# Four w3·w_out sums open at once, six places for w3, and 40 products on zeros ahead of the first head

## The chip, the cores and the metric

The kernel runs on one core of a Trainium2 chip. The metric is the device time of one execution in microseconds (us), the median of three runs. Of the kernel before, one execution was also taken by the hardware profiler; every duration below comes from that one.

The core has five engines that run queues of their own, in order: PE (TensorE: matrix products, whose weight loads are listed apart as PEld), DVE (VectorE), ACT (ScalarE), POOL (GpSimd) and SP (SyncE, which here only starts DMA transfers). An instruction waits for semaphores that other engines or transfers raise; everything behind it on its queue waits too.

## What is computed

Attention with a band and 32 global tokens over 8 batches of 8 heads, and behind it a gated block on the attention's 4,352 rows:

```python
# per head: 512 local and 32 global queries, head_dim 64
s_g  = scale * q_g @ k_all.T                 # global tokens see all
s_ll = where(|i - j| <= 32, scale * q_l @ k_l.T, -1e9)
s_l  = concat([scale * q_l @ k_g.T, s_ll])
out  = concat([softmax(s_g) @ v_all, softmax(s_l) @ concat([v_g, v_l])])
# all heads of a token side by side: x is (8*544) x 512
a = x @ w1;  b = x @ w2                      # 512 x 1024 each
h = a * b @ w3                               # 1024 x 1024
y = h @ w_out                                # 1024 x 512
```

The kernel folds `w3 @ w_out` into one 1024 x 512 matrix first (called w34), so that the gated product is multiplied once. Weights arrive as 64-bit words, which ACT and DVE turn into 32-bit floats; products that need it are done with a high and a low part of an operand.

## The kernel before, in words

**The early part.** The weights come in units of 512 KB (16 of `w3`, 8 of `w_out`, 8 of `w12`, the latter holding w1 and w2 side by side) and in 16 half units (`w12s`). A unit is fetched into one of three `raw` buffers (`fetch`), unpacked in three steps (`unit`: step 0 on DVE, step 2 on ACT, step 3 on DVE), and for w12 split into high and low (steps 4 and 5). `fold(t, j)` is one product of 128 rows of w3's tile t with 128 rows of w_out; eight of them, j = 0 to 7, add up to a 128-row block t of w34 in one PSUM bank, and the trace shows each as two MATMUL instructions. Eight blocks make 64 folds. `fold(t, j)` needs the half tile of w3 (t, j // 4) and the unit j of w_out. A finished block is copied out as a high part (`w34h`, ACT) and a low part (`w34l`, DVE).

**A head n** is loaded (`kr`, `qr`, by pairs `vr`), split (`kh`, `kl`, `qs`, `vs`), scored (`s`, eight products), put through maximum (`mmax`, DVE), exponent (`exps`, ACT) and scaling by the inverse sum (`norm`, ACT or DVE), transposed (`t`), split into `PTh`, `PTl` and `G` on ACT and DVE, multiplied with v (`av`, ten products) and added up (`cb`, ACT; `sum`, DVE). The global tokens take `sg` (scores, by pairs of heads) and `tg` (transposes, by four heads). When the four pairs of a batch are there, `first` (12 products each; tiles `ap` and `bp`), a gate and `second` (tile `acc`) make the gated block; that goes on beside the heads of the next batches.

**What sets the order.** Nothing is scheduled on the chip. A planner in the program (`list_schedule`) goes through all steps with costs and due times that are written by hand, and its answer is the order in which each engine's instructions stand. `ORDER` lists the weight units, `W0 + WD * n` is the due time of the n-th, `LA` is the distance of the first eight heads, `LB` that of the later ones. `take(tag, bufs, ...)` tells the planner how many places a tile has. Before, `product(t)` puts the eight folds of one block one behind the other, w3 has two places (`w3f`), and `ORDER` brings the whole of w_out ahead of w3's tiles 1 to 7.

**The very front.** POOL clears `QG` (the high and low parts of the global queries, 128 x 512) before ACT casts the first queries into it.

## Time and profile before

| | us |
|---|---|
| median of three runs | 936.43 (933.89 to 937.55) |
| the profiled execution | 934.75 |
| its span in the trace | 933.0 |
| PE busy | 871.0 (93%) |
| ACT busy | 667.2 (72%) |
| DVE busy | 636.5 (68%) |
| POOL busy | 385.4 (41%) |

The profiled execution lies 1.7 us under the median, inside the range of the three runs. What the span does not cover of it is 1.75 us. A stretch is read by the busy time of its engines and by the clock that TensorE was granted (1.00 is 2.4 GHz, 0.5 is 1.2 GHz, and a value between is the mean of a stretch that had both). Where PE is not busy, the view of waits and the timeline name what it waited for. From 215 us to 800 us PE is busy in 99 of 100 us at the full clock, so that stretch is as long as its products.

### The profile page before, as it was taken

How to read it: one execution, taken by the hardware profiler on the slowest of the kernel's cores; microseconds unless marked ns; L12 is line 12 of the kernel's file. 1: busy time of each engine (PE TensorE's matmuls, PEld its weight loads, DVE VectorE, ACT ScalarE, POOL GpSimd, SP SyncE). 2: the span in 40 equal slices, each digit the busy share in tenths (PEclk: the TensorE clock that was granted, in tenths of full speed). 3: DMA queues.
4: the chain of work that ended last, by engine and by line, in shares of the span. 5: the costliest groups of instructions: out<-in, count | busy, mean ns of one | idle time of the engine just before them, and what ended most of it. 6: DMA issues, size and time to landing. Idle time of an engine off the chain costs nothing.

```text
span 933.0 us, 17736 instructions
## 1 busy us (share of the span) xinstructions
PE 871.0 (93%) x6016; PEld 786.1 (84%) x6016; DVE 636.5 (68%) x1683; ACT 667.2 (72%) x1779; POOL 385.4 (41%) x462
## 2 busy tenths in 40 slices
PE   3599968799999999999999999999999999999995
PEld 2355548688999999999999999999999999999994
DVE  4779887886777868786878677878786767512111
ACT  5678887897878787878887888788878877512111
POOL 4444457554544345444544454345434543200000
PEclk9789968999999999999999999999999999999998
DMA  9755533423131313131313231223121211000000
GB/s 270 238 157 162 180 122 125 140 81 90 54 100 40 98 48 105 46 99 54 98 53 95 57 99 52 85 62 94 49 89 57 91 45 36 1 23 23 1 23 22
DMA packets 38514, 78.51 MB, mean 84 GB/s; under 512 B 5784, under 2 KB 6808, under 8 KB 38424
## 3 DMA queue, kind: packets, MB, share of 16 engines
q1 hardware_dynamic: 38424, 77.39, 27.2%
q8 instruction: 47, 0.77, 0.3%
q14 instruction: 43, 0.35, 0.1%
HBM read 68.45 MB, written 8.91 MB: 83 GB/s over the span
## 4 chain that ended last, share of the span: by engine, by line
PE 79%; ACT 8%; DVE 6%; DMA 3%; issue 2%; POOL 1%; SPq 0%; ACTq 0%; POOLq 0%; DVEq 0%
PE bp L495 7%; PE bp L496 7%; PE bp L497 7%; PE acc L525 6%; PE acc L527 6%; PE acc L526 6%; PE ap L497 5%; PE ap L495 5%; PE ap L496 5%; PE w L630 5%; PE s L299 4%; PE av L379 3%; PE av L378 3%; DVE PTl L233 3%; PE t L325 3%; ACT PTh L230 2%
## 5 line engine op out<-in xcount | busy, mean ns | idle before, releaser
L495 PE MATMUL ap<-x,w12h 128*128 128x256 f32 x544 | 158.4, 291 | 0.6 <-ACT w12h L230 0.6
L497 PE MATMUL ap<-x,w12l 128*128 128x256 f32 x544 | 155.2, 285 | 1.3 <-POOL w12l L233 1.2
L495 PE MATMUL bp<-x,w12h 128*128 128x256 f32 x544 | 155.1, 285 | 0.0
L496 PE MATMUL ap<-x,w12h 128*128 128x256 f32 x544 | 154.5, 284 | 0.0
L496 PE MATMUL bp<-x,w12h 128*128 128x256 f32 x544 | 154.3, 284 | 0.0
L497 PE MATMUL bp<-x,w12l 128*128 128x256 f32 x544 | 154.2, 284 | 0.0
L307 ACT ACTIVATE P<-P,mn 128x192 f32<-128x192 f32 (+1 forms) x256 | 121.2, 475 | 13.0 <-DVE mn L303 11.5
L233 DVE TENSOR_TENSOR PTl<-t,PTh 32x96 fp32r<-32x96 f32 (+1 forms) x192 | 76.6, 399 | 76.9 <-ACT PTh L230 39.9
L233 POOL TENSOR_TENSOR kl<-kr,kh 128x608 fp32r<-128x608 f32 x56 | 84.7, 1513 | 101.2 <-ACT kh L230 81.3
L230 ACT CAST PTh<-t 32x96 fp32r<-32x96 f32 (+1 forms) x192 | 66.8, 348 | 59.2 <-PE t L328 34.1
L497 PEld LDWEIGHTS ap<-x,w12l 128*128 128x128 f32 x544 | 104.5, 192 | 2.2 <-POOL w12l L233 1.9
L496 PEld LDWEIGHTS bp<-x,w12h 128*128 128x128 f32 x544 | 104.4, 192 | 2.0
L495 PEld LDWEIGHTS bp<-x,w12h 128*128 128x128 f32 x544 | 104.4, 192 | 1.9
L495 PEld LDWEIGHTS ap<-x,w12h 128*128 128x128 f32 x544 | 104.7, 192 | 0.9 <-ACT w12h L230 0.8
L496 PEld LDWEIGHTS ap<-x,w12h 128*128 128x128 f32 x544 | 104.8, 193 | 0.1
L497 PEld LDWEIGHTS bp<-x,w12l 128*128 128x128 f32 x544 | 104.4, 192 | 0.0
L303 DVE CUSTOM_DVE_ANT_0 P<-s,cs 128x192 f32<-128x192 f32 (+1 forms) x256 | 86.0, 387 | 6.5 <-PE s L299 4.8
L233 POOL TENSOR_TENSOR qs<-qr,qs 64x512 fp32r<-64x512 f32 x46 | 61.9, 1346 | 49.7 <-ACT qs L230 37.3
L630 PE MATMUL w<-wo,w3f 128*128 128x512 f32 x128 | 64.4, 642 | 13.9 <-DVE wo L556 12.3
L299 PE MATMUL s<-kh,qs 128*128 128x192 f32 (+1 forms) x256 | 67.1, 296 | 5.3 <-POOL qs L233 2.8
L401 DVE TENSOR_TENSOR u<-av,cb 64x704 f32<-64x704 f32 x64 | 56.8, 887 | 19.2 <-ACT cb L394 18.4
L379 PE MATMUL av<-PTl,vs 128*128 128x192 f32 (+1 forms) x256 | 65.6, 280 | 0.0
(785 smaller groups left out, 2377.8 us busy)
## 6 DMA issues: line engine op xcount, KB each, us to landing
kr<-in_kd_t_dram SPq DMA_DIRECT2D x128, 152.0 KB, 2.9
raw_w<-in_w_t_dram SPq DMA_DIRECT2D x24, 512.0 KB, 4.1
kpr<-in_kp_t_dram SPq DMA_DIRECT2D x32, 272.0 KB, 2.8
out_dram<-o SPq DMA_DIRECT2D x34, 256.0 KB, 2.9
qr<-in_q_t_dram SPq DMA_DIRECT2D x64, 128.0 KB, 2.7
vr<-in_v_t_dram SPq DMA_DIRECT2D x32, 256.0 KB, 2.7
raw_wo<-in_wo_t_dram SPq DMA_DIRECT2D x8, 512.0 KB, 6.3
raw_w12s<-in_w_t_dram SPq DMA_DIRECT2D x16, 256.0 KB, 3.3
```

The lines of the kernel that those rows point to most:

```text
L230: (nc.scalar.copy if eng in (None, nc.scalar) else eng.tensor_copy)(dst, src)
L233: (eng or nc.gpsimd).tensor_sub(dst, src, f(hi))
L299: nc.tensor.matmul(st[:, e, 0:w], qs[:, 128 * e : 128 * e + 128], kk[:, o : o + w], start=(j == e % 2 == 0), stop=(j == 1), skip_group_che ...
L303: nc.vector.tensor_tensor_reduce(blk(n, e), T["st", n][:, e, 0 : WIN[e][1]], masks[e], -0.125, 3.0e38, ALU.add, ALU.min, T["mn", n][:, e : ...
L307: nc.scalar.activation(blk(n, e), blk(n, e), AF.Exp, bias=T["mn", n][:, e : e + 1], scale=-1.0, accum_out=T["sm", n][:, e : e + 1])
L379: nc.tensor.matmul(dst, v, PTl[:, j, c0:c1], start=False, stop=last, skip_group_check=True)
L401: nc.vector.tensor_add(u[r : r + 64], T.pop(("av", n))[r : r + 64, :, 0:352], T.pop(("cb", n))[r : r + 64])
L495: nc.tensor.matmul(d, wh[:, k, c, :], x[:, 0, 0:w], start=(k == m % 2 == 0), stop=False, skip_group_check=True)
L496: nc.tensor.matmul(d, wh[:, k, c, :], x[:, 1, 0:w], start=False, stop=False, skip_group_check=True)
L497: nc.tensor.matmul(d, wl[:, k, c, :], x[:, 0, 0:w], start=False, stop=(k == 3), skip_group_check=True)
L525: nc.tensor.matmul(a, gh[:, m % 2, sl], wh, start=(m == 0), stop=False)
L630: nc.tensor.matmul(T["w34", t], T["w3f", t, j // 4][:, j % 4], T["wo"][:, j], start=(j == 0), stop=(j == 7))
```

## The change

It has four parts.

1. `ORDER` is rewritten: w3's tiles 0 to 3 (first halves) alternate with w_out's units 0 to 3, then their second halves with w_out's units 4 to 7; tiles 4 to 7 follow as before. `W0` goes from -16 to -8, `WD` from 3.0 to 2.6, `LA` from 8 to 9.
2. The blocks 0 to 3 of w34 accumulate at the same time, in four PSUM banks (two of `acc`, and the banks `a` and `b` that `first` uses later). Each fold now has the due time of its own two units.
3. w3's half tiles get six places: two of `w3f`, and four buffers (`g`, `as`, `gh`, `gl`) that the gate uses later.
4. `halves`: 40 products, 256 columns wide, on `QG` while it holds zeros, as PE's first work; 8 use all 128 rows, 32 use rows 0 to 63 and 64 to 127 in turn and two banks in turn. Nothing reads what they write.

```diff
-LA, LB, LF = 8.0, 11.2, 4.0
+LA, LB, LF = 9.0, 11.2, 4.0
-W0, WD = -16.0, 3.0
+W0, WD = -8.0, 2.6
 ORDER = (
-    ('w3', 0, 0), ('wo', 0, 0), ('wo', 1, 0), ('wo', 2, 0), ('wo', 3, 0), ('w3', 0, 1), ('wo', 4, 0), ('wo', 5, 0),
+    ('wo', 0, 0), ('w3', 0, 0), ('w3', 1, 0), ('wo', 1, 0), ('w3', 2, 0), ('wo', 2, 0), ('w3', 3, 0), ('wo', 3, 0),
...
+W3F = ("w3f", "w3f", "g", "as", "gh", "gl")
+W34P = ("acc", "acc", "a", "b")
...
-                    T["w3f", a, h] = P["early"].tile([128, 4, 128], F32, tag="w3f", name=f"w3f{a}_{h}", bufs=2)
+                    tag = W3F[[u[1:] for u in ORDER if u[0] == "w3"].index((a, h)) % len(W3F)]
+                    pool, n = (P["early"], 2) if tag == "w3f" else (p1, 1)
+                    T["w3f", a, h] = pool.tile([128, 4, 128], F32, tag=tag, name=f"w3f{a}_{h}", bufs=n)
...
     def fold(t, j):
         if j == 0:
-            T["w34", t] = ps_acc.tile([128, 512], F32, tag="acc", name=f"w34_{t}")
+            tag = W34P[t % 4]
+            T["w34", t] = (ps_acc if tag == "acc" else ps_1).tile([128, 512], F32, tag=tag, name=f"w34_{t}")
...
+    def halves():
+
+        z = QG.rearrange("p a b -> p (a b)")
+        st = ps_1.tile([128, 2, 512], F32, tag="s", name="halves")
+        for r in range(8):
+            nc.tensor.matmul(st[:, 0, 0:256], z[:, 128 * (r % 2) : 128 * (r % 2) + 128], z[:, 256:512],
+                             start=True, stop=True)
+        for r in range(32):
+            h, c = 64 * (r % 2), 128 * (r // (2 if r < 16 else 4) % 2)
+            nc.tensor.matmul(st[:, r % 2, 0:256], z[h : h + 64, c : c + 128], z[h : h + 64, 256:512],
+                             start=True, stop=True)
...
-    def product(t, due):
-        take("acc", 2, ("w34", t), ("fold", t, 0))
+    def product(t):
+        due = {u: W0 + WD * n for n, u in enumerate(ORDER)}
+        due = [max(due["w3", t, j // 4], due["wo", j, 0]) + 4.0 for j in range(8)]
+        tag = W34P[t % 4]
+        take(tag, W34P.count(tag), ("w34", t), ("fold", t, 0))
...
-            add(("fold", t, j), only("PE", COST["fold"]), due + 0.1 * j, deps, fold, t, j)
+            add(("fold", t, j), only("PE", COST["fold"]), due[j], deps, fold, t, j)
...
+    add(("halves",), only("PE", 4000), -70.0, [("clear", "QG")], halves)
```

**Where it moves instructions: the front of ACT.** Before, ACT's first instructions (the names in brackets are semaphores that an instruction waits for, `PE_49` being the one that PE raises):

```order
L230 ACT_TABLE_LOAD [waits DMAHW0_49]
L230 CAST QG_77<-qgr0_97 64x4x32 [waits Pool_49]
L230 CAST QG_77<-qgr0_97 64x4x32
L554 ACTIVATE raw_w30_0_101<-raw_w30_0_101 128x512 [waits DMAHW2_49]
L554 ACTIVATE raw_wo0_0_103<-raw_wo0_0_103 128x512 [waits DMAHW3_49]
L230 CAST qs0_146<-qr0_106 64x512 [waits DMAHW4_49]
L554 ACTIVATE raw_wo1_0_108<-raw_wo1_0_108 128x512 [waits DMAHW5_49]
L230 CAST vgs_76<-vgr0_112 64x8x64 [waits DMAHW7_49,DMAHW6_49]
L230 CAST kh0_164<-kr0_119 128x608 [waits DMAHW1_49,DMAHW0_49]
```

and after the change:

```order
L233 ACT_TABLE_LOAD [waits DMAHW0_49,PE_49]
L233 CAST QG_77<-qgr0_97 64x4x32 [waits Pool_49]
L233 CAST QG_77<-qgr0_97 64x4x32 [waits PE_49]
L233 CAST qs0_163<-qr0_142 64x512 [waits DMAHW2_49]
L233 CAST vgs_76<-vgr0_144 64x8x64 [waits DMAHW4_49,DMAHW3_49]
L233 CAST kh0_176<-kr0_148 128x608 [waits DMAHW6_49,DMAHW5_49]
L557 ACTIVATE raw_wo0_0_156<-raw_wo0_0_156 128x512 [waits DMAHW7_49]
```

ACT's first instruction now waits for PE (the products of `halves` read `QG`, which ACT is to overwrite), and two of the three scalings of weight units that stood ahead of head 0's `kh` stand behind it.

**PE around the transposes of head 1.** Before, from the folds ahead of `t1` on (`w34_0`, `w34_1` are blocks of w34, `w3f0_1` is the second half of w3's tile 0):

```order
L630 MATMUL w34_0_152<-wo_93,w3f0_1_273 128x512 x2
L325 MATMUL t1_392<-cs_70,P1_72 128x128 x4
L328 MATMUL t1_392<-cs_70,P1_72 128x128 x3
L630 MATMUL w34_0_152<-wo_93,w3f0_1_273 128x512
L422 MATMUL sg2_438<-kph2_390,QG_77 128x272 x2
L422 MATMUL sg2_438<-kpl2_407,QG_77 128x272 x2
L382 MATMUL av1_446<-G_75,vgs_76 128x288
```

and after:

```order
L636 MATMUL w34_2_408<-wo_93,w3f2_0_386 128x512 x2
L636 MATMUL w34_0_261<-wo_93,w3f0_0_254 128x512
L636 MATMUL w34_1_281<-wo_93,w3f1_0_272 128x512
L636 MATMUL w34_2_408<-wo_93,w3f2_0_386 128x512
L328 MATMUL t1_439<-cs_70,P1_72 128x128 x4
L331 MATMUL t1_439<-cs_70,P1_72 128x128 x3
L636 MATMUL w34_3_453<-wo_93,w3f3_0_437 128x512 x3
L636 MATMUL w34_0_261<-wo_93,w3f0_0_254 128x512
L385 MATMUL av1_485<-G_75,vgs_76 128x288
```

Between the value products of head 0 and those of head 1 stood three folds, all of block 0; now nine stand there, of four blocks. Before `t1`, 9 folds are done where 6 were.

**ACT around the copy `cb7` of head 7.** Before:

```order
L230 CAST kh9_1195<-kr9_827 128x608
L307 ACTIVATE P0_71,sm8_1177<-P0_71,mn8_1176 128x192
L307 ACTIVATE P0_71,sm8_1177<-P0_71,mn8_1176 128x256 x2
L307 ACTIVATE P0_71,sm8_1177<-P0_71,mn8_1176 128x192
L230 CAST w12h1_84<-raw_w121_0_1074 128x512
L394 COPY cb7_1226<-av7_1207 64x704
```

and after:

```order
L233 CAST w12h2_86<-raw_w122_0_1165 128x512
L557 ACTIVATE raw_w122_1_1204<-raw_w122_1_1204 128x512
L233 CAST kh9_1251<-kr9_973 128x608
L233 CAST qs9_1266<-qr9_1025 64x512
L310 ACTIVATE P0_71,sm8_1225<-P0_71,mn8_1224 128x192
L310 ACTIVATE P0_71,sm8_1225<-P0_71,mn8_1224 128x256
L397 COPY cb7_1280<-av7_1255 64x704
```

Ahead of `cb7` ACT now works on w12's tile 2, where it was at tile 1. In all, 222 steps of the planner stand ahead of `cb7` on ACT where 208 stood: eight more `norm`, three more scalings and two more high parts of w12 units, two more copies of `tg`, one more `qs`, and two `exps` fewer.

## Rows read from the trace of the kernel before

**Rows 1.** Busy time by stretch: stretch, length, PE PEld DVE ACT POOL (instructions), clock, DMA, GB/s.

```profile
0.00:14.00 14.00, 3.15 (x4) 1.04 (x5) 4.06 (x9) 5.85 (x10) 6.47 (x11) 1.00 0.86 232
14.00:51.00 37.00, 21.68 (x88) 15.65 (x87) 27.58 (x82) 26.06 (x69) 15.66 (x15) 0.76 0.81 245
51.00:121.00 70.00, 68.26 (x260) 38.35 (x260) 58.41 (x150) 57.53 (x151) 35.66 (x42) 0.98 0.53 166
121.00:139.00 18.00, 9.21 (x44) 7.60 (x43) 14.42 (x36) 15.40 (x41) 10.07 (x12) 0.63 0.42 134
139.00:215.00 76.00, 67.33 (x454) 60.88 (x454) 61.26 (x149) 62.82 (x171) 43.74 (x49) 0.93 0.37 115
215.00:800.00 585.00, 579.08 (x4329) 549.15 (x4328) 443.49 (x1212) 471.98 (x1285) 267.96 (x326) 1.00 0.23 70
```

**Rows 2.** Waits of PE, 0 to 62 us: total us, times, longest.

```profile
PE w L630 <- DVE wo L556: 12.3, 3, 10.0
```

**Rows 3.** Timeline of the front: start us, us, engine, line, what, [idle before <- releaser].

```profile
0.74 0.52 POOL L187 MEMSET QG<- 128x512 f32 x1 [0.29 <-POOLq L1046]
2.56 1.28 ACT L230 ACT_TABLE_LOAD   x1 [2.56 <-DMA qgr<-in_qg_t_dram]
3.85 0.62 ACT L230 CAST QG<-qgr 64x128 fp32r<-64x128 f32 x2
...
13.15 0.70 ACT L230 CAST kh<-kr 128x608 fp32r<-128x608 f32 x1 [0.48 <-DMA kr<-in_kd_t_dram]
13.88 0.79 DVE L233 TENSOR_TENSOR kl<-kr,kh 128x608 fp32r<-128x608 f32 x1 [1.01 <-ACT kh L230]
14.01 1.15 PE L299 MATMUL s<-kh,qs 128*128 128x192 f32 x1
```

**Rows 4.** Timeline of PE: neighbouring 256-column products, of head 0 and of head 3.

```profile
15.65 0.41 PE L299 MATMUL s<-kh,qs 128*128 128x256 f32 x1
15.87 0.41 PE L299 MATMUL s<-kl,qs 128*128 128x256 f32 x1
...
58.00 0.28 PE L299 MATMUL s<-kl,qs 128*128 128x256 f32 x1
58.12 0.28 PE L299 MATMUL s<-kh,qs 128*128 128x256 f32 x1
```

**Rows 5.** Timeline of ACT and PE: the key cast and first score product of head 1.

```profile
26.02 0.70 ACT L230 CAST kh<-kr 128x608 fp32r<-128x608 f32 x1 [0.15 <-DMA kr<-in_kd_t_dram]
...
30.08 0.34 PE L299 MATMUL s<-kh,qs 128*128 128x192 f32 x1
```

**Rows 6.** Timeline of PE: its last long waits in the early part, and the folds behind.

```profile
36.33 0.58 PE L382 MATMUL av<-G,vgs 128*128 128x288 f32 x1 [5.10 <-DVE PTl L233]
...
47.62 0.79 PE L422 MATMUL sg<-kph,QG 128*128 128x272 f32 x2 [3.80 <-DVE mn L303]
...
50.77 4.34 PE L630 MATMUL w<-wo,w3f 128*128 128x512 f32 x6
```

**Rows 7.** Timeline of PE: four folds (eight instructions) at the full clock.

```profile
102.24 3.62 PE L630 MATMUL w<-wo,w3f 128*128 128x512 f32 x8
```

**Rows 8.** ACT's groups, 0 to 215 us: count, busy us, mean ns, idle before.

```profile
L307 ACT ACTIVATE P<-P,mn 128x192 f32<-128x192 f32 (+1 forms) x56 | 26.4, 473 | 4.7 <-DVE mn L303 4.4
L554 ACT ACTIVATE raw_w<-raw_w 128x512 f32<-128x512 f32 x24 | 15.7, 674 | 2.6 <-DMA raw_w<-in_w_t_dram 2.5
...
L317 ACT ACTIVATE P<-P,sm 128x192 f32<-128x192 f32 (+1 forms) x34 | 14.5, 472 | 0.0
...
L230 ACT CAST w12h<-raw_w 128x512 fp32r<-128x512 f32 x8 | 5.2, 656 | 0.1
```

**Rows 9.** Waits of PE, 121 to 215 us, the two longest groups.

```profile
PE av L382 <- ACT P L307: 3.1, 1, 3.1
PE s L299 <- POOL qs L233: 2.8, 1, 2.8
```

**Rows 10.** Timeline: copy `cb` of head 7 on ACT, first product of `first` on PE.

```profile
130.15 0.74 ACT L394 COPY cb<-av 64x704 f32<-64x704 f32 x1 [1.05 <-PE av L379]
...
138.92 0.47 PE L495 MATMUL ap<-x,w12h 128*128 128x256 f32 x1
```

More of the change, by code (lines that the diff above doesn't have):

```diff
@@ L48 @@
 SEEN, SEEN_PE, ISSUE, LAND, RATE = 110, 300, 480, 1900, 270.0
-LA, LB, LF = 8.0, 11.2, 4.0
+LA, LB, LF = 9.0, 11.2, 4.0
 HOLD_A, HOLD_D, HOLD_P = 400, 0, 90000
-W0, WD = -16.0, 3.0
+W0, WD = -8.0, 2.6
 ORDER = (
-    ('w3', 0, 0), ('wo', 0, 0), ('wo', 1, 0), ('wo', 2, 0), ('wo', 3, 0), ('w3', 0, 1), ('wo', 4, 0), ('wo', 5, 0),
-    ('wo', 6, 0), ('wo', 7, 0), *[('w3', t, e) for t in range(1, 8) for e in range(2)],
-    *[('w12', m, e) for m in range(MA) for e in range(2)],
-)
+    ('wo', 0, 0), ('w3', 0, 0), ('w3', 1, 0), ('wo', 1, 0), ('w3', 2, 0), ('wo', 2, 0), ('w3', 3, 0), ('wo', 3, 0),
+    ('w3', 0, 1), ('wo', 4, 0), ('w3', 1, 1), ('wo', 5, 0), ('w3', 2, 1), ('wo', 6, 0), ('w3', 3, 1), ('wo', 7, 0),
+    *[('w3', t, e) for t in range(4, 8) for e in range(2)], *[('w12', m, e) for m in range(MA) for e in range(2)],
+)
+W3F = ("w3f", "w3f", "g", "as", "gh", "gl")
+W34P = ("acc", "acc", "a", "b")
 def list_schedule(steps, after):
@@ L929, in weight @@
         if kind == "w3":
-            take("w3f", 2, ("w3f", a, e), me[3])
+            tag = W3F[[x[1:] for x in ORDER if x[0] == "w3"].index((a, e)) % len(W3F)]
+            take(tag, W3F.count(tag), ("w3f", a, e), me[3])
         if kind[:3] == "w12":
@@ L936, in weight @@
             read(me[5], ("raw", *u))
-    def product(t, due):
-        take("acc", 2, ("w34", t), ("fold", t, 0))
+    def product(t):
[3 more added lines that the diff above has]
+        take(tag, W34P.count(tag), ("w34", t), ("fold", t, 0))
         for j in range(8):
             deps = [("unit", "w3", t, j // 4, 3), ("unit", "wo", j, 0, 3)] + [("fold", t, j - 1)] * (j > 0)
-            add(("fold", t, j), only("PE", COST["fold"]), due + 0.1 * j, deps, fold, t, j)
+            add(("fold", t, j), only("PE", COST["fold"]), due[j], deps, fold, t, j)
             read(("fold", t, j), ("w34", t), ("w3f", t, j // 4))
-        add(("w34h", t), only("ACT", COST["w34h"]), due + 2, [("fold", t, 7)], fold_split, t, 0)
-        add(("w34l", t), only("DVE", COST["w34l"]), due + 3, [("w34h", t)], fold_split, t, 1)
+        add(("w34h", t), only("ACT", COST["w34h"]), due[7] + 2, [("fold", t, 7)], fold_split, t, 0)
+        add(("w34l", t), only("DVE", COST["w34l"]), due[7] + 3, [("w34h", t)], fold_split, t, 1)
         read(("w34h", t), ("w34", t))
@@ L967, in band_attention_glu_kernel @@
     for t in range(8):
-        product(t, W0 + WD * (8 + 2 * t) + 4.0)
+        product(t)
     for b in range(B):
```

## The prediction

> **What bounds the kernel now.** I read first the busy times of the engines and the granted clock by stretch [rows 1]. From 215 us to 800 us PE is busy 579.1 of 585 us at the full clock, and the order of the work there is the same in both programs. So the change is worth what it saves before 215 us, and all of that reaches the end. Before 215 us PE stands still for 10.9, 15.3, 1.7, 8.8 and 8.7 us in the five stretches, 45 us in all. On top of that comes the low clock: a granted clock c means that (1-c)/0.5 of the stretch ran at 1.2 GHz, where a product takes twice as long. That is 0.48 x 21.7/2 = 5.2 us in 14 to 51, 0.74 x 9.2/2 = 3.4 in 121 to 139, 0.14 x 67.3/2 = 4.7 in 139 to 215, and with 0.04 x 68.3/2 = 1.4 in between some 15 us. So 60 us are there to be won at most.
>
> Then I read what PE waited for. In 0 to 62 us the largest group is folds that wait for a unit of w_out [rows 2]; two long waits on its queue follow, of 5.10 us for head 0's weights and of 3.80 us for a maximum [rows 6]. From 50.8 us on PE is fed: 51 to 121 is 68.3 of 70 us busy, because folds are left over to fill it. After 121 us the folds are used up and PE waits for ACT's exponents and POOL's splits [rows 9]; ACT is 15.4 of 18 us busy there and 62.8 of 76 behind it, DVE 14.4 and 61.3 [rows 1]. So there are three regions: transfers and in-order waits up to 51, PE itself up to 121, ACT with DVE up to 215. The change moves folds out of the second into the first; what it does to ACT's order decides the third.
>
> **The front: 40 products.** They start when POOL has cleared QG, at 1.26 us [rows 3], say 1.4. PE had nothing until 9.95 us, so on PE they cost nothing; their cost is that ACT's first instruction now waits for their end, E. Behind it are queued the table load, both casts of QG, and the casts of head 0's q, of the global v and of head 0's k; DVE's low parts wait for those, PE's first scores for DVE, and SP's load of q2 (a place in a ring of three) for DVE's low part of q0. No row shows a product on 64 rows, so I bound it. Two neighbours of 256 columns are 0.22 us apart at the low clock and 0.12 at the high one [rows 4]. All 40 one after the other at the low clock take 8.8 us (E = 10.2); if two halves run at the same time and the clock is high throughout, 8 + 16 steps of 0.12 take 2.9 us (E = 4.3). A gain on PE is excluded, since they add work that nothing uses. For the clock the nearest rows are those of the run of PE that begins at 47.62 after a wait: at 50.77 its six fold instructions take 4.34 us where 2.7 would do at the full clock, so the low clock lasted there to about 54.1, 6.5 us from the start of the run [rows 6]. By that, 29 products run at the low clock and 11 at the high one if they go one by one (6.4 + 1.3, E = 9.1), and all 24 steps at the low clock if the halves go two at a time (5.3, E = 6.7). No row is nearer to the one than to the other; I take the middle, E = 7.9.
>
> The Trainium skill's page "TensorEngine Tiling (Array Packing)", section "Key Properties", says that tiles of different rows load and multiply in parallel, and that a change of tiling mode drains the engine. No run here shows either. By the first sentence E would be 6.7 instead of 7.9, and the sum below would be 1.2 us better; with halves one by one it would be 1.2 us worse.
>
> From E to head 0's first score stand the table load 1.28, two QG casts 0.62, casts of q, v and k of about 0.6, 0.6 and 0.70, and DVE's low part of k 0.79 [rows 3], with the hand-overs 4.9 us: 12.8 us, where it was 14.0 [rows 3]. So the products eat up most of what the earlier loads of head 0 bring, and no more.
>
> **Head 1.** Before, its key cast waited for its load until 26.0 us [rows 5]. Ahead of that load stand 2.1 MB less now (three full and two half weight units fewer); at 232 to 245 GB/s [rows 1] it lands some 9 us sooner, near 17. That is early enough: ACT is now last. From head 0's scores to ACT's first exponent I count 2.5 us (eight products at the low clock 1.7, the first maximum and hand-overs 0.8), then ACT has 16 instructions up to and with head 1's key cast, between 0.40 and 0.70 us each (exponents 0.473, scalings of units 0.674, of rows 0.472 [rows 8]), 8.7 us; POOL's low part adds 1.5. Head 1's scores start at 12.8 + 2.5 + 8.7 + 1.5 + 0.2 = 25.7, where it was 30.1 [rows 5].
>
> **Up to the point where PE is fed.** Behind head 1's scores stand 8 + 5 products of 0.12, two folds, 7 products. A fold is two instructions of 3.62/8 = 0.45 us [rows 7], so 0.9. Head 0's transposes end at 25.7 + 1.6 + 1.8 + 0.8 = 29.9. From there to head 0's value products it was 6.2 us (30.1, where head 1's scores followed the transposes [rows 5], to 36.3 [rows 6]) and the splits between are the same: 36.1. That is the last long wait, because behind it stand nine folds up to head 1's value products where three stood; their units (w_out 2 and 3, w3's tiles 2 and 3) come before or shortly after by the queue. Before, PE was fed from 50.8 us, and had by then done three folds, one sg, one t and two av more: 2.7 + 31 products x 0.12 = 6.4 us. So the same work was reached at 44.4 and is now reached at 36.1: **8.3 us won**. The slow clock at the start of the fed stretch (six instructions in 4.34 us where 2.7 would do [rows 6]) is paid in both.
>
> **What is given back while PE is fed.** With four blocks open, every step j needs a new unit of w_out and two to four folds follow; the units come at DVE's pace, which was 58.4 of 70 us busy [rows 1]. I give 2.0 us for short waits ahead of j = 4 to 7, from none (in the whole stretch PE stood still for 1.7 us before [rows 1], whatever it waited for) to 4 (eight units at 0.5). Places and banks cost nothing: the four buffers and two banks are first needed by the gate, behind 138.9 us [rows 10], and the folds end near 113.
>
> **ACT behind the folds.** Ahead of head 7's copy ACT gets 14 steps more: eight scalings of rows 3.8, three of units 2.0, two high parts 1.3, two copies 0.8, a q cast 0.6, less two exponents of 0.473 + 0.19: 7.2 us [rows 8]. Head 7's copy ran at 130.15 and `first` began at 138.9 [rows 10]; ACT is the last there, so nearly all of the 6.2 us left is given back at that place. But 3.3 us of the 7.2 is work on w12 that ACT did later before, and 1.9 of the row scalings come back too (over the whole program it is four more, not eight): 5.2 us returns in 139 to 215, where PE waits today. What stays on ACT is four scalings and a copy, 2.5 us. In return DVE loses those, about 2 us; since DVE was nearly as busy as ACT there, I count half, 1.0.
>
> **Sum**: -8.3 + 2.0 + 2.5 - 1.0 = -4.8 on 934.75, with the bounds of E shifting it by +2.3 or -3.6 (nearly one for one until the load at 17 us is last). Clock: PE idles less in 14 to 36 us, and of the 5.2 us lost there I count 0.5 as saved. That makes **-5.3, 929.5** for the profiled execution. It lay 1.7 us under the median; on the median of 936.4 it is **931.1**.
>
> **The rivals.**
> - *The lull keeps it*: ACT's 7.2 us more ahead of head 7 are not returned by 215 us, because the later heads wait for ACT in turn. For it: ACT is 82 to 86% busy from 121 on, the highest of the helpers [rows 1]. Against: the w12 work done early is missing later. Then -8.3 + 2.0 + 7.2 - 1.0 = -0.1: 936 on the median, between 932 and 940.
> - *Slower*: ACT is held at the front by all 40 products one after the other at the low clock (E = 10.2, +2.3), and is last from there on. Then the folds win nothing, since what PE waits for is ACT's casts at every head: the 8.3 us fall away, and the 7.2 us stand in full, less what DVE gives: 934.75 + 2.3 + 7.2 - 1.0 = 943 (945 on the median). It decides when ACT's idle time of 0 to 139 us (8.2, 10.9, 12.5 and 2.6 in the four stretches [rows 1]) doesn't fall by at least 7 us.
> - *The whole gain stays*: the halves run two at a time (E = 6.7, -1.2), no waits for units, and w12 being ready earlier saves 3 of the 8.7 us that PE stands still in 139 to 215: -8.3 - 1.2 - 3 = -12.5, 924 on the median, down to 920.
> - *The sums stand open, but PE isn't fed*: units come too late for four blocks at once (4 us instead of 2.0 and more), which leads to the first rival's time.
>
> **How the numbers follow.** What a measurement of this kernel can tell from no change is about 0.5%, 4.7 us. I give the forecast (926 to 933.5) 0.47, of which 0.34 lies under 931.7; the whole gain 0.11; the lull, with units too late, 0.25; slower by ACT 0.17. Faster by over 0.5%: 0.34 + 0.11 = 0.45. Within 0.5%: 0.13 + 0.25 = 0.38. Slower: 0.17. The range is 923 to 941: left out are about half of the whole gain and most of the slower case.
>
> **What would show it.** The table load on ACT starts near 7.9 us (4.3 to 10.2); head 0's scores near 13, head 1's near 26 with the key cast no longer waiting for a transfer; head 0's value products near 36 and no wait over 2 us on PE behind them until the last fold, which ends near 113 instead of 121, where the fed stretch ended; `first` begins between 134 and 139; from there PE is busier than 67.3 of 76 us. If head 1's scores come at 30 or later, the front is wrong; if the last fold ends near 113 and the end is still 936, the lull has kept it; if folds wait for w_out throughout, the open sums are not fed.

## The result and the profile after

The changed kernel takes 939.92 us (median of 18 runs, 936.98 to 942.78), the kernel before beside it 935.46 (18 runs, 933.67 to 937.67). The ratio is 1.0047, with an interval from 1.0036 to 1.0058: 4.5 us slower by the medians, just inside the 0.5% that the prediction called no change, and 8.8 us over its forecast of 931.1, which was faster. The profiled execution of the changed kernel took 941.34 us, its span is 939.6.

Busy time by stretch of the changed kernel, in the columns of [rows 1]:

```profile
0.00:14.00 14.00, 8.01 (x52) 7.34 (x52) 4.99 (x7) 4.71 (x8) 6.63 (x11) 0.81 0.78 237
14.00:51.00 37.00, 26.70 (x91) 14.82 (x91) 27.79 (x75) 27.92 (x74) 15.05 (x13) 0.79 0.86 225
51.00:121.00 70.00, 64.39 (x246) 36.66 (x244) 59.46 (x143) 58.75 (x154) 35.30 (x42) 0.95 0.59 180
121.00:139.00 18.00, 7.72 (x31) 6.24 (x31) 15.49 (x34) 16.41 (x42) 11.88 (x11) 0.61 0.50 160
139.00:215.00 76.00, 66.09 (x432) 60.69 (x433) 56.10 (x147) 59.28 (x168) 46.25 (x56) 0.89 0.31 91
215.00:800.00 585.00, 578.78 (x4325) 548.72 (x4325) 440.37 (x1205) 470.72 (x1281) 274.24 (x331) 1.00 0.25 72
```

PE's idle time fell in 14 to 51 us from 15.3 to 10.3 us. It rose in all three stretches behind: from 1.7 to 5.6, from 8.8 to 10.3 and from 8.7 to 9.9, and the granted clock fell in each of them. The steady stretch from 215 us on is what it was.

The front, as a timeline (start us, us, engine, line, what, [idle before <- releaser]):

```profile
1.32 2.08 PE L650 MATMUL halves<-QG 128*128 128x256 f32 x8 [1.32 <-POOL QG L190]
3.33 3.05 PE L654 MATMUL halves<-QG 64*128 64x256 f32 x32
6.46 1.28 ACT L233 ACT_TABLE_LOAD   x1 [6.46 <-PE halves L654]
9.43 0.69 ACT L233 CAST kh<-kr 128x608 fp32r<-128x608 f32 x1
10.18 0.53 PE L302 MATMUL s<-kh,qs 128*128 128x192 f32 x1 [3.80 <-ACT kh L233]
...
33.94 0.58 PE L385 MATMUL av<-G,vgs 128*128 128x288 f32 x1 [3.58 <-DVE PTl L236]
...
36.18 6.12 PE L636 MATMUL w<-wo,w3f 128*128 128x512 f32 x10
```

The 32 half products take 3.05 us, the eight full ones ahead of them 2.08. The table load waits for them until 6.46. Head 0's scores start at 10.18 (14.01 before [rows 3]), its value products at 33.94, and from the folds at 36.18 on PE is fed.

What PE waited for behind that, as the timeline shows it:

```profile
47.59 1.13 PE L636 MATMUL w<-wo,w3f 128*128 128x512 f32 x2 [1.95 <-DVE wo L559]
...
58.73 0.37 PE L385 MATMUL av<-G,vgs 128*128 128x288 f32 x1 [1.83 <-DVE PTl L236]
...
61.73 6.19 PE L636 MATMUL w<-wo,w3f 128*128 128x512 f32 x8
...
123.89 0.73 PE L328 MATMUL t<-cs,P 128*128 128x128 f32 x2 [4.04 <-ACT P L320]
...
130.92 0.58 PE L385 MATMUL av<-G,vgs 128*128 128x288 f32 x1 [2.46 <-DVE PTl L236]
...
138.91 1.49 PE L328 MATMUL t<-cs,P 128*128 128x128 f32 x4 [4.34 <-ACT P L320]
```

The eight fold instructions at 61.73 take 6.19 us, where 3.62 do at the full clock [rows 7]; the last folds end at 117.5 us (120.3 before). The transposes of heads 7 and 8 wait 4 us each for ACT's scaling of rows, and the first product of `first` starts at 142.49 (138.92 before [rows 10]).

**An account of PE's lost time.** Busy time counts slow products in full, so I also keep an account that does not: for a milestone (the scores, transposes or values of a head) I take the time at which PE starts it, less the full-clock length of all that stands ahead of it in PE's order. The lengths are distances between starts in the trace of before, once PE is fed: scores 1.0 us, transposes 0.68, values 1.16, `sg` 0.53, `tg` 0.55, a fold 0.9, twelve products of `first` or a `second` 1.44; products that nobody reads count nothing. What is left is what PE lost up to there, interpolated between milestones. Only differences between kernels mean something, and each account is of one execution: kernels whose orders are the same up to about 119 us differ by up to 0.9 us at 51, 1.7 at 80 and 0.6 at 121.

| lost up to, us | 51 | 80 | 121 | 139 | 160 | 200 | 250 |
|---|---|---|---|---|---|---|---|
| before | 35.6 | 37.6 | 38.1 | 51.0 | 57.8 | 66.7 | 69.0 |
| after | 29.4 | 36.7 | 39.0 | 52.8 | 60.0 | 71.6 | 73.0 |

So the change is 6.2 us ahead at 51 us, 0.9 ahead at 80, 0.9 behind at 121, 2.2 behind at 160, 4.9 at 200 and 4.0 at 250. The value at 121 needs care: that time lies inside the 4.04 us that PE waits ahead of head 7's transposes, and the interpolation spreads this wait over both its sides. At the scores of head 7 (near 114 us in both) the account stands at 36.0 against 37.8, so the change is still 1.8 us ahead there; at the transposes of head 7 it stands at 41.1 against 37.9. The lead is lost in that wait. The experiments ask what ate the 6.2, and what took 4 more.

### The profile page after: what moved, and what is told of

The parts are those of the page before. It is cut to its first block, busy times and chain, and to the rows that moved or that the text cites. A ratio compares the mean times of both kernels' runs of the same rounds, so it can differ in the third digit from the quotient of the medians.

```text
span 939.6 us, 17828 instructions
## 1 busy us (share of the span) xinstructions
PE 880.4 (94%) x6056; PEld 793.7 (84%) x6056; DVE 634.8 (68%) x1665; ACT 668.7 (71%) x1785; POOL 396.8 (42%) x474
## 4 chain that ended last, share of the span: by engine, by line
PE 77%; ACT 9%; DVE 7%; DMA 3%; issue 2%; POOL 1%; SPq 0%; ACTq 0%; DVEq 0%; POOLq 0%
PE bp L498 7%; PE bp L500 7%; PE bp L499 6%; PE acc L528 6%; PE acc L530 6%; PE acc L529 6%; PE ap L498 5%; PE ap L499 5%; PE ap L500 5%; PE s L302 4%; DVE PTl L236 3%; PE w L636 3%; PE av L382 3%; PE av L381 3%; PE t L328 3%; ACT PTh L233 2%
## 5 line engine op out<-in xcount | busy, mean ns | idle before, releaser
L236 POOL TENSOR_TENSOR kl<-kr,kh 128x608 fp32r<-128x608 f32 x57 | 86.6, 1520 | 89.0 <-ACT kh L233 71.6
L233 ACT CAST PTh<-t 32x96 fp32r<-32x96 f32 (+1 forms) x192 | 66.8, 348 | 62.8 <-PE t L331 36.7
L404 DVE TENSOR_TENSOR u<-av,cb 64x704 f32<-64x704 f32 x64 | 56.8, 887 | 23.9 <-ACT cb L397 23.1
L302 PE MATMUL s<-kl,qs 128*128 128x192 f32 (+1 forms) x256 | 64.8, 287 | 1.7 <-DVE kl L236 0.9
```

The costliest lines, as they stand in the source:

```text
L233: (nc.scalar.copy if eng in (None, nc.scalar) else eng.tensor_copy)(dst, src)
L236: (eng or nc.gpsimd).tensor_sub(dst, src, f(hi))
L302: nc.tensor.matmul(st[:, e, 0:w], qs[:, 128 * e : 128 * e + 128], kk[:, o : o + w], start=(j == e % 2 == 0), stop=(j == 1), skip_group_che ...
L404: nc.vector.tensor_add(u[r : r + 64], T.pop(("av", n))[r : r + 64, :, 0:352], T.pop(("cb", n))[r : r + 64])
```

## The experiments

Ratios are to the kernel before, timed beside each. Where due times or the places known to the planner change (experiments 2 and 4, the heads at 8 us, and the two kernels with an order made for four buffers), the planner wrote a new order; elsewhere the order was kept, but for what the edit moves.

**1. The products alone.** One kernel leaves them out of the changed program, one puts them into the kernel before.

```diff
+            if k == ("halves",):
+                continue
```

> The changed kernel with its 40 products on zeros left out and every other instruction in the same place. The changed kernel's trace has them end at 6.4 us, and ACT's table load starts at 6.46, 3.9 us later than before the change. Theory (the loss arises behind the folds, in ACT's order for heads 6 to 9, and in waits for units between 50 and 80 us): head 0's scores start some 2 us sooner, the transfers then bound head 1, and the end moves by no more than 1 us: ratio to the kernel before 1.003 to 1.005. Rival (the products hold ACT at the front and the delay is carried to the end): the end comes 3 to 4 us sooner, ratio 1.000 to 1.002.

> The kernel before with the 40 products added right behind POOL's clearing of QG, all else in its place. ACT's table load then waits until about 6.5 us. Theory: the transfer of head 0's key lands at 13.1 us in the kernel before, so ACT has caught up by then and the end moves by less than 1 us: ratio 0.999 to 1.001. Rival (they hold ACT): 3 to 4 us later, ratio 1.003 to 1.004.

Measured: 940.08 us without them, ratio 1.0047 [1.0031, 1.0064]; the kernel before with them 935.48, ratio 1.0004 [0.9992, 1.0016]. Without them head 0's scores start at 8.21 instead of 10.18, the transposes of head 8 at 136.8 instead of 138.9, and at 250 us 0.9 us of it is left. They cost nothing that the runs can tell in either program, and ACT being held at the front is not the cause. That a start 2 us earlier is worth nothing at the end is the first sign that something else sets the pace.

**2. The due numbers and the open sums, apart.** The kernel before with the new numbers, and the changed kernel with the old ones.

```diff
-LA, LB, LF = 9.0, 11.2, 4.0
+LA, LB, LF = 8.0, 11.2, 4.0
-W0, WD = -8.0, 2.6
+W0, WD = -16.0, 3.0
```

> The kernel before with only the three numbers LA 9, W0 -8, WD 2.6: blocks one after the other, old order of the units, no products on zeros. Theory (the numbers put the w12 units ahead of heads 6 to 9 on ACT, and this is what loses): the transposes of heads 6 to 8 wait for ACT's scalings again and it is slower than before, ratio 1.003 to 1.008. Rival (the open sums lose by their waits for units of w_out): no change or faster, 0.997 to 1.001.

> The changed kernel with the old numbers LA 8, W0 -16, WD 3.0: four sums open, new order of units, products on zeros. Theory (the numbers lose): faster than the changed kernel by 3 to 6 us, ratio 0.996 to 1.001. Rival (the open sums lose): as slow as the changed kernel or slower, 1.004 or more.

Measured: 941.66 us, 1.0066 [1.0046, 1.0086], for the new numbers alone; 950.11, 1.0156 [1.0143, 1.0169], for the open sums with the old numbers. In the second, head 1's scores come at 33.3 us and the last fold ends at 130.2. In the first, head 0's scores come at 7.8 us and head 1's at 21.6, so the numbers bring the first heads forward without the open sums, but the account at 51 us stays at 35.4. Neither half is the good one: each alone is slower than the two together, at 1.0047.

**3. Single waits taken away.** A fourth raw buffer, in the place of w12's last low half, which is empty until then; the scalings of rows of heads 6 to 9 left out; the last sixteen folds moved back; heads due every 8 us.

```diff
-            raw = P["early"].tile([128, 512, 2], I32, tag="raw", name=name, bufs=3)
+            fourth = ORDER.index((kind, a, e)) % 4 == 3 and kind != "w12"
+            pool, tag, n = (P["w12a"], "w12l3", 1) if fourth else (P["early"], "raw", 3)
+            raw = pool.tile([128, 512, 2], I32, tag=tag, name=name, bufs=n)
```

> The changed kernel with four buffers for the raw units of w3 and w_out in place of three (the fourth is the place of the last w12's low half, which is empty until then); the order of every instruction is kept. Theory A, the units come late for want of raw buffers: the folds' waits for DVE between 44 and 80 us (1.95 and 1.14 us) go, t_6 (112.2 us) comes 3 to 4 us sooner and the time is 935.5 to 937.5. Theory B, heads 6 to 9 are late because w12's units are put ahead of them on ACT and DVE: the folds' waits may go, but t_8 stays within 1 us of 138.9 and the time is 939 to 940.5.

```diff
+            if k[0] == "norm" and k[1] in (6, 7, 8, 9):
+                continue
```

> The changed kernel without the 16 normalizations of heads 6 to 9 (left out, so the output of these heads is not normalized); everything else in its order. Theory B (the transposes of heads 7 and 8 wait 4.0 and 4.3 us for ACT's normalizations, which stand behind the scalings of w12's units): both waits shrink to below 2.5, t_8 comes at 133 to 135.5 in place of 138.9, and the time is 934 to 936.5. Theory A (what is lost is lost before 80 us): t_8 gains at most 1.5 us and the time is 938 to 940.

```diff
+MOVED = (
+    ([("fold", 6, j) for j in range(8)] + [("w34h", 6), ("w34l", 6)], ("s", 7)),
+    ([("fold", 7, j) for j in range(4)], ("t", 7)),
+    ([("fold", 7, j) for j in range(4, 8)] + [("w34h", 7), ("w34l", 7)], ("av", 7)),
+)
```

> The changed kernel with the 16 products of the last two sums moved back in the order: the sum of block 6 behind the scores of head 7, that of block 7 in two halves behind the transposes and the values of head 7; all else in its order. Theory C (heads 6 to 8 are late because the folds stand ahead of t_6 on TensorE, and the lull at 121 to 139 us lacks the folds that filled it before): t_6 comes at 107 to 110 in place of 112.2, last fold ends at 128 to 132, time 934 to 937.5. Theory B (ACT and DVE set when heads 6 to 8 are ready, whatever TensorE does): t_6 comes sooner by at most 2 us, t_8 stays at 137.5 to 139.5, time 938.5 to 941.

```diff
-LA, LB, LF = 9.0, 11.2, 4.0
+LA, LB, LF = 8.0, 11.2, 4.0
```

> The changed kernel with the due time of a head at 8.0 us per head as before in place of 9.0; the due numbers of the units (-8 and 2.6) stay. Theory B (the lost time is heads put behind w12's units by the due numbers): t_6 at 105 to 108, t_8 at 131 to 134, time 932 to 936. Theory A or C: the units come later still against the heads, the sums end later (119 to 123), and the time is 938 to 943.

Measured: 939.07 us, 1.0041 [1.0026, 1.0056], with the fourth buffer; 939.73, 1.0049 [1.0031, 1.0067], without the scalings; 955.4, 1.0209 [1.0190, 1.0228], with the folds moved back; 943.81, 1.0088 [1.0073, 1.0102], with the heads at 8 us.

The edits moved what they name, mostly by less than expected, and none of it reached the end. The first two times lie in the ranges of theory B (four buffers) and theory A (no scalings), the other two above every range. Waits of ACT for transfers in 51 to 80 us, first of the changed kernel, then with four raw buffers (engine, what <- releaser: total us, times, longest):

```profile
ACT raw_w L557 <- DMA raw_w<-in_w_t_dram: 2.6, 1, 2.6
```

```profile
ACT raw_w L557 <- DMA raw_w<-in_w_t_dram: 0.5, 1, 0.5
```

The transfer comes sooner, but PE's folds still wait for DVE, 2.4 us for a unit of w_out and 1.3 for one of w3 in 44 to 80 us (1.9 and 1.1 in the changed kernel), and head 6's transposes stay at 112.2. I take it that the units stand on DVE between the heads' work, and not before a missing buffer; no run shows it alone. Without the scalings of rows, the same two transposes of heads 7 and 8 wait for the engine that is next late:

```profile
123.48 0.66 PE L328 MATMUL t<-cs,P 128*128 128x128 f32 x4 [2.30 <-DVE u L404]
127.81 0.50 PE L302 MATMUL s<-kh,qs 128*128 128x192 f32 x1 [3.34 <-DVE mg L440]
131.97 0.58 PE L385 MATMUL av<-G,vgs 128*128 128x288 f32 x1 [2.17 <-DVE PTl L236]
137.79 1.09 PE L328 MATMUL t<-cs,P 128*128 128x128 f32 x4 [2.31 <-DVE u L404]
```

The releasers are now DVE's, and the four waits sum to 10.1 us where three summed to 10.8: ACT gave way, and DVE, which is busy 16.3 of 18 us there, took its place. With the folds moved back, the transposes of head 6 come at 108.0 as expected (112.2), but w34 is finished at 148 us, and in the program the half units of w12 have to wait for it. With the heads due every 8 us, head 8's transposes come at 136.3, not at 131 to 134, since the units are later against the heads, and the account stands at 70.7 us at 190 and 75.5 at 200 (66.7 before).

**4. The weights against the heads.** In the changed order ACT scales 30 large units ahead of head 8's last exponent where it scaled 27, so w12's units were given later due times (in the third kernel together with the fourth buffer, made known to the planner).

```diff
-        weight(u, W0 + WD * n)
+        weight(u, W0 + WD * n if n < 24 else 63.0 + 3.375 * (n - 24))
```

> The changed kernel with the eight large units of w12 due at 63.0 + 3.375 per unit (8.6 to 14 us later) and nothing else changed. In the order of ACT one of them moves behind head 8 (29 large units ahead of it in place of 30, 27 in the kernel before) and five small ones behind head 10 (3 in place of 8, 3 before). Theory E, ACT and DVE are the bound up to 139 us and every unit put ahead of a head pushes that head back by its 1.4 to 1.9 us of their work, which gives nothing back after 139 us: t_8 at 136.5 to 138 (138.9), the first gate product at 140 to 141.5 (142.5), t_10 at 168 to 171 (173.9), time 935 to 938. Rival F, the order of the weights against the heads is not what costs (the small losses sit in the front's missing stock of products): t_8 within 1 us, time 938.5 to 941.

> The same, with the eight units due 7 us later still (70.0 + 3.375 per unit): 28 large units ahead of head 8 on ACT, 31 ahead of head 10. Theory E: t_8 at 135 to 136.5, first gate product at 138.5 to 140, t_10 at 166 to 169, time 932 to 936, unless the gate products then wait for w12 (a wait of ap for w12l over 2 us in 139 to 215 us), which gives back the same. Rival F: 938.5 to 942.

> The first of these two (units of w12 due from 63.0 on) with a fourth raw buffer for the units of w3 and w_out, which the order is made for as well: 25 large units ahead of head 6 in place of 22. Theory E: units ahead of head 6 cost as they do ahead of head 8, t_6 comes 2 to 4 us later than in the first of these, and the time is 1 to 3 us over it. Rival F: the folds' waits between 44 and 80 us (1.95 and 1.14 us) go and the time is 1 to 4 us under it.

Measured: 939.84 us, 1.0048 [1.0027, 1.0069]; 943.3, 1.0077 [1.0057, 1.0097]; 939.21, 1.0042 [1.0026, 1.0057]. The middle term of theory E held better than expected: head 8's transposes come at 135.2 and 133.0 us (138.9), the first gate product at 138.6 and 137.0 (142.5), head 10's transposes at 170.6 and 161.2 (173.9). The end did not follow. In the second kernel (its trace is of the fastest of six executions, 939.86 us), waits of PE in 139 to 215 us:

```profile
PE av L385 <- DVE PTl L236: 4.3, 2, 3.0
PE acc L528 <- ACT gh__1959 L233: 3.5, 1, 3.5
PE ap L498 <- ACT w12h L233: 1.9, 2, 1.0
PE ap L500 <- DVE w12l L236: 1.6, 1, 1.6
PE ap L500 <- POOL w12l L236: 1.3, 2, 0.9
```

Now the gate products wait for w12 (4.8 us in the last three rows; 0.7 in the changed kernel), the exception that theory E had named. Heads or weights are late, by whichever is put second. In the third kernel head 6's transposes come at 112.1, 0.8 us later than in the first and not 2 to 4, and its time is the same: neither theory named what is left.

**5. ACT and DVE sooner, and the clock.** Two kernels have the fourth raw buffer and an order made for it, one of them the changed kernel with the old distance of heads and of w12's units, the other the kernel before. Two more fill PE's waits with products that nobody reads.

```diff
-        weight(u, W0 + WD * n)
+        weight(u, W0 + WD * n if n < 24 else 56.0 + 3.0 * (n - 24))
```

> The changed kernel with a fourth raw buffer that the order is made for, heads due every 8.0 us as before, and the eight large units of w12 due from 56.0 on, 3.0 apart, as before. Theory H, ACT and DVE set the pace up to 139 us and the changed front did not bring their work forward (89 and 90 us of it done by 121 us before, 91 and 92 after): here their work comes 4 us or more forward by 80 us and the heads are not put back, so the first gate product comes at 134 to 137 and the time is 929 to 934. Rival J, the loss only changes its place whatever is brought forward: 937 to 943.

> The kernel before with the same fourth raw buffer and an order made for it; nothing else. Theory H: DVE and ACT have 2 us or more of work done sooner by 80 us (55 and 54 before) and the time is 931 to 934.5. Rival J: within 1 us of the kernel before (934.5 to 936.5), or slower.

```diff
+            if k in FILL:
+                fill(FILL[k])
...
+        for _ in range(n):
+            nc.tensor.matmul(T["fill"], W34[0][0][:, 0:128], W34[0][0], start=True, stop=True)
```

> The changed kernel with 43 products of 512 columns that nobody reads (0.25 us each at the higher clock) in five places where TensorE waits between 119 and 157 us: 14 ahead of the transposes of head 7, 8 ahead of its values, 15 ahead of the transposes of head 8, 3 ahead of its values, 3 ahead of the transposes of head 9. Theory G, the idle pieces cost a second time by the lower clock (granted 0.61 from 121 to 139 us, 0.83 to 160, 0.90 to 190): the clock is granted at 0.9 or more from 121 to 190 us, the products behind run 4 to 6 us sooner in sum, and the time is 935 to 938. Rival: the gate products are held by ACT and DVE as long as by the clock, so 939 to 941; slower than 941 if the fillers hold back the work behind them.

> The kernel before with 35 such products between 121 and 151 us (5 ahead of the scores of head 8, 11 ahead of the values of head 7, 3 ahead of the transposes of head 8, 9 ahead of the scores of head 9, 7 ahead of the transposes of head 9). Theory G: the clock, granted 0.63 and 0.83 in 121 to 139 and 139 to 160 us, is 0.9 or more, and the time is 931 to 933.5. Rival: 934.5 to 937.

Measured: 941.5 us, 1.0063 [1.0045, 1.0081]; 947.79, 1.0123 [1.0101, 1.0145]; 940.02, 1.0048 [1.0030, 1.0067]; 935.77, 0.9996 [0.9985, 1.0006].

Theory H falls. In the first of these DVE and ACT have 60.6 and 61.3 us of work behind them at 80 us, where the kernel before has 54.9 and 54.3, the first gate product comes at 137.5, and the time is worse. The second kernel is no test of it: DVE and ACT have 53.4 and 55.0 us of work done at 80 us, so nothing was brought forward there, and the new order loses 40.9 us by 80 and 79.8 by 250 (37.6 and 69.0 before). Theory G falls too, for the stretch that was filled. The changed kernel with the filling products, 121 to 139 and 139 to 160 us:

```profile
121.00:139.00 18.00, 12.70 (x68) 9.42 (x67) 16.37 (x36) 17.13 (x44) 12.59 (x12) 1.00 0.50 160
139.00:160.00 21.00, 16.70 (x112) 14.75 (x110) 13.89 (x30) 13.50 (x37) 14.42 (x17) 0.92 0.30 88
```

The clock is granted in full where it was 0.61. The first gate product comes at 139.8 us in place of 142.5 (0.8 of this is there at head 6's transposes, ahead of the fillers), but the transposes of heads 9 and 10 at 156.6 and 173.4, as they did (156.4 and 173.9). The slow products of this stretch lay beside waits for other engines, and what they gave back was lost again within 20 us.

**6. The order behind the sums.** The account of these kernels:

| lost up to, us | 51 | 80 | 121 | 139 | 160 | 200 | 250 |
|---|---|---|---|---|---|---|---|
| w12 latest | 29.4 | 36.1 | 38.7 | 49.7 | 56.3 | 71.6 | 74.4 |
| fourth buffer, old distances | 26.5 | 34.4 | 38.1 | 50.1 | 56.8 | 70.7 | 73.6 |
| after, waits filled | 28.6 | 36.0 | 38.8 | 52.1 | 59.9 | 71.2 | 72.6 |
| before, waits filled | 36.5 | 38.4 | 38.7 | 50.2 | 56.3 | 66.9 | 69.2 |

Two things stand out. At 121 us these four and the two of the first table lie between 38.1 and 39.0, whatever they had at 51, between 26.5 and 36.5 (at head 7's scores, ahead of the wait that 121 us falls into, they are still apart, at 35.2 to 38.7). And at 200 us the changed orders lie between 70.7 and 71.6, though two of them were 1.0 and 1.5 us ahead of the kernel before at 160. So the order behind the sums was changed by itself: one kernel up to the low half of its last sum, then the remaining steps as the other has them.

```diff
-        for _, n, e in list_schedule(steps, after):
+        for key, e in json.loads(zlib.decompress(base64.b85decode(SEQUENCE))):
+            n = where[json.dumps(key)]
```

> The changed kernel up to the low half of its last sum (the first 589 steps of its order, buffers and all), and from there on every remaining step in the order and on the engines of the kernel before. Theory K, the order behind the sums is what costs: the loss between 139 and 200 us falls from 18.8 us back to 15 to 16.5, and the time is 934.5 to 937. Theory L, the first 120 us leave head 7 and what follows late, and no order behind makes it good: 938.5 to 941.

> The reverse: the kernel before up to the low half of its last sum (610 steps), and the remaining steps in the order and on the engines of the changed kernel. Theory K: the loss between 139 and 200 us rises from 15.7 to 18 or more, and the time is 937.5 to 941. Theory L: within 1 us of the kernel before, 934.5 to 936.5.

> The order of the run with the fourth raw buffer and the heads due as before up to the low half of its last sum (631 steps), and the remaining steps as the kernel before has them. That run was 0.9 us ahead of the kernel before at 139 us and 4.0 behind at 200. Theory K: 933 to 936. Theory L: 938 to 942.

| front | order behind | us | ratio | lost 139 to 200 |
|---|---|---|---|---|
| before | before | 935.56 | 1 | 15.7 |
| before | after | 942.96 | 1.0083 [1.0070, 1.0096] | 19.7 |
| after | before | 937.95 | 1.0034 [1.0021, 1.0047] | 16.9 |
| after | after | 939.92 | 1.0047 [1.0036, 1.0058] | 18.8 |
| fourth buffer | before | 937.87 | 1.0024 [1.0015, 1.0033] | 17.3 |
| fourth buffer | its own | 941.5 | 1.0063 [1.0045, 1.0081] | 20.6 |

The order behind costs 7.4 us with the front of before and 3.6 with the front with four buffers. With the changed front the medians differ by 2.0 us, but these two were timed apart, their ratios differ by 0.13% (1.2 us), and the intervals overlap: that one is not clear of the noise. Theory K is right on the sign in the first two, and not contradicted in the third. On the size it was too low with the front of before (937.5 to 941 expected), and too hopeful with the two others: 937.95 and 937.87 lie between its ranges and those of theory L, so the fronts leave something behind too. The changed front with the order of before keeps a wait of the change: its steps up to the last sum bring ACT's work ahead of head 7's transposes with them.

```profile
123.46 1.62 PE L490 MATMUL t<-cs,P 128*128 128x128 f32 x4 [3.64 <-ACT P L482]
```

The other waits go with the order. Waits of PE in 139 to 215 us, the front of before with the order of after, and then the front of after with the order of before:

```profile
PE t L488 <- ACT P L480: 5.9, 3, 4.3
PE av L545 <- DVE PTl L396: 3.8, 4, 1.5
PE s L462 <- DVE mg L600: 1.7, 1, 1.7
PE bp L658 <- DVE g__1528 L668: 1.4, 1, 1.4
PE bp L658 <- DVE g__1735 L668: 1.1, 1, 1.1
```

```profile
PE s L464 <- POOL qs L398: 3.3, 1, 3.3
PE t L490 <- ACT P L482: 2.4, 1, 2.4
PE av L547 <- DVE PTl L398: 1.3, 2, 0.8
PE ap L660 <- ACT w12h L395: 1.0, 1, 1.0
```

The changed kernel itself, and then the kernel before, have in the same stretch and view:

```profile
PE t L328 <- ACT P L320: 5.6, 3, 4.3
PE av L385 <- DVE PTl L236: 2.8, 4, 0.9
PE s L302 <- DVE mg L440: 2.2, 1, 2.2
PE bp L498 <- DVE g__1569 L508: 1.8, 1, 1.8
PE bp L498 <- DVE g__1776 L508: 1.0, 1, 1.0
```

```profile
PE t L325 <- ACT P L317: 2.2, 1, 2.2
PE acc L525 <- ACT gh__1727 L230: 2.1, 1, 2.1
PE av L382 <- DVE PTl L233: 1.2, 2, 0.6
```

Transposes behind ACT's scalings for 5.6 to 5.9 us, values for 2.8 to 3.8, and gate products behind DVE's gate twice: these rows come with the order of after under either front. With the order of before the first two are at 2.4 and 1.3 (2.2 and 1.2 in the kernel before), and the gate rows are gone; the 3.3 us for `qs` is a wait that the kernel before has too, 2.8 us [rows 9], just ahead of 139 us.

The front's own sign depends on what follows: it wins 3.0 us with its own order behind it (942.96 to 939.92) and loses 2.4 with that of before (935.56 to 937.95). No kernel here beats the kernel before.

## Why the prediction was wrong

- **The front: right in kind, and better than the sum.** E was put at 7.9 us between 4.3 and 10.2; the table load starts at 6.46. The two-at-a-time branch of the working (6.7) was the nearer one. The Trainium skill's page "TensorEngine Tiling (Array Packing)", section "Key Properties", says that tiles of different rows multiply in parallel; the trace agrees, the two halves of a pair start within 5 ns of each other. Head 0's scores came at 10.2 (12.8 forecast) and head 1's at 22.2 (25.7). Part of this is that the first product waited for ACT's key cast alone (3.7 us from E, where 4.9 were counted), and that all three scalings of weight units, not two, moved behind that cast.
- **PE fed from 36.1: sooner.** The 36.1 was the start of head 0's value products, and they start at 33.94; that the folds behind them start at 36.18 is chance. Still the 8.3 us won were only 6.2 in the account at 51 us: the first ten fold instructions took 6.12 us where 4.5 would do, and the folds at 47.59 waited 1.95 us for a unit of w_out.
- **Given back while PE is fed, 2.0 (0 to 4): mis-sized.** By the account 5.3 us of the lead went between 51 and 80, and at head 7's scores 1.8 of 6.2 were left: 4.4 to 5.3 where 2.0 was put, just over the bound of 4. The last fold ended at 117.5, not near 113. The stock of folds that fed PE from 51 us on before had been paid for by PE's long wait in the front. The change spent it as it came, so the folds wait for units (1.9 and 1.1 us) and the values for DVE (1.8), and the eight fold instructions at 61.73 run 2.6 us longer than at the full clock. The term was worked out from waits per unit; the trace of before held a hint. DVE and ACT had 31.6 and 31.9 us of work done at 51 us before and 32.8 and 32.6 after: the engines that make the units gained only about 1 us from a front in which PE gained 6. That this is what limits the stretch is argued: with 5.7 and 7.0 us more of their work done at 80 us, the kernel with four buffers was no faster.
- **ACT behind the folds, 6.2 given up and 5.2 returned: the step that failed.** The first half held: head 7's transposes waited 4.04 us for ACT, and `first` began 3.6 us later. The work that had moved ahead was missing later, as counted: from 139 to 215 us ACT's busy time fell from 62.8 to 59.3 and DVE's from 61.3 to 56.1. But that gave PE nothing, its own busy time fell as well, from 67.3 to 66.1, and the account loses 3.1 us more from 139 to 200 than before. This is the step that turned the sign: from head 7's scores to 250 us the account went from 1.8 ahead to 4.0 behind, 5.8 us where the sum had 2.5 less 1.0 (7.2 less 5.2 would be 2.0, not 2.5; that changes nothing here). Work taken off two engines was counted as time returned to a third, without asking which row of waits it shortens. The planner had written a new order for that stretch, and its waits were longer. The order from the last sum on is one part of it: with the old order put back there, 2.4 us of the loss stay, and the wait ahead of head 7's transposes with them.
- **Clock, 0.5 saved: wrong in sign.** By the working's own formula the low clock took 5.6 us in 14 to 51 (5.2 before) and 3.2 in 51 to 121 (1.4 before), where PE is fed; no run tried what that cost. From 121 to 139 us it was no cost that reached the end: raised to 1.00 there, the time stayed.
- **The rivals.** The lull that keeps it (936, from 932 to 940) comes nearest in mechanism, with the time at its upper end. ACT held by the products falls with the first experiment, though the sign that the prediction gave for it came true: ACT's idle time up to 139 us fell by 3.0 us, not by 7. That sign could not tell the two apart.

**Open.** The spans of the profiled executions differ by 6.6 us, the account at 250 us by 4.0 and the medians by 4.5. The 2.6 us between the first two lie behind 250 us; the kernel with four raw buffers in the unchanged order has only 0.8 there, so I do not count them to the change. Why the account stands at 38.1 us or more at 121 us in every kernel, that is, what makes PE wait there for head 7 or head 8 whatever the front has won, is not settled: a fourth raw buffer, leaving out the products at the front, or more of DVE's and ACT's work done by then (95.6 and 94.7 us with four buffers, 90.1 and 89.4 before) did not bring it lower. With ACT's scalings of rows left out, PE waited for DVE at the same places, so neither engine alone is shown to be the limit. Why the planner's order behind the sums is worse, by which of its costs, was not tried either.

## What to carry to other kernels

Time won on the engine that is fed was lost again here, while the engines that feed it had got ahead by 1 us; in one run they were ahead by 6 to 7 us, and that was not enough either. Before counting a gain at the front, compare how far *they* are at its end, and name the next wait that the gain has to pass. When a planner writes the order, an edit of due times rewrites stages that it never names; put the old order behind the new front (and the reverse) to see which of the two is paid for. Of the changed orders tried here, each one was slower, by 0.2 to 2.1%: an edit that shortens one wait has to be weighed against an order in which the waits already fit together.

## What the runs showed of the hardware

- Products on 64 rows that alternate between rows 0 to 63 and 64 to 127, and between two banks, run two at a time: in the trace of the changed kernel the two of a pair start within 5 ns of each other, and one pair follows the other after 0.21 us, the same step as between the products on 128 rows just ahead of them. From 5.4 us on the step is 0.12 us, that of the higher clock in [rows 4].
- The change from one form to the other is not free: around 3.33 us two steps are 0.35 and 0.38 us long where 0.21 is the rule, some 0.3 us in all. (The first step after PE's idle start, at 1.32 us, is 0.38 us long too.)
- Filling PE's waits raised the granted clock from 0.61 to 1.00 between 121 and 139 us, and in the kernel before from 0.63, and neither kernel got faster by more than the noise (940.02 against 939.92, 935.77 against 936.26): a low clock beside waits for other engines can be a symptom alone. Where PE is fed, the slow products themselves take longer: eight fold instructions at 61.73 us took 6.19 us in place of 3.62, at a granted clock of 0.59 from 61.7 to 67.9 us. Whether that reaches the end was not tried.
